# One issue order for the whole kernel, with PSUM banks and elu's buffers named in it, in a fused linear attention and ELU feed-forward kernel

## The chip, the cores and the metric

The kernel runs on one core of one Trainium2 chip. The metric is the device time of one execution in microseconds, taken as the median of several runs. Engines are named as in the profile: PE is TensorE's matmuls, PEld its weight loads, DVE is VectorE, ACT is ScalarE, POOL is GpSimd, SP is SyncE, whose queue issues most DMAs. L704 is line 704 of the kernel before.

## The reference

For four batches of eight heads, 768 steps and a head of 48, a state of 48 x 48 is decayed by row and updated at each step, and read out; the output, as 3072 tokens of 384, goes through a feed-forward layer with ELU. All is float32.

```python
state = alpha[:, :, t, :, None] * state + einsum('bhd,bhe->bhde', k[:, :, t], v[:, :, t])
y[:, :, t] = einsum('bhd,bhde->bhe', q[:, :, t], state)
...
h = x @ w_in                                   # 384 -> 2048
g = where(h > 0, h, exp(minimum(h, 0)) - 1)
out = g @ w_out                                # 2048 -> 384
```

## The kernel before

**Windows.** The attention goes in 24 windows of 128 steps (6 per batch). A window is made by steps with names of their own, called tokens; i is the window. L loads q, k and alpha, LV loads v (both on SP's queue). SC scans alpha into a running product P, LN and EX make its inverse R, KA, KB and KC scale k by it (KC with a Newton step), SQ scales q, PC adds up a check. T (or TP on PE with KN on ACT) transposes k. S multiplies k by q in blocks of 64 steps, MK masks that. U multiplies k by v, UA, UB and UC carry the state (UC's result is the next window's). Y multiplies the state and the masked scores into y; XH rounds y to the upper half in float32r, XL is the rest, and XD moves 32 rows of both by two DMAs into xt, the block's input of the feed-forward.

**Feed-forward.** It goes in 9 blocks of tokens, three of 256 (two windows each) and six of 384 (three windows each), and in 16 parts j of 128 hidden units (8 pairs of parts for the narrow blocks). A(b,j) are the matmuls into a PSUM bank h, nine (or 18) for the three products upper x upper, upper x rest, rest x upper. RA and RB (ACT) make exp(min(h,0)), RC (DVE) the ELU, GH (ACT) its upper half, GL the rest. O(b,j) multiplies both into the two or three output banks, Z copies a bank out on ACT and stores it. A(b,.) needs all of block b's windows, XD too.

**Weights.** F loads a packed weight, DA, KW and DB unpack it, WH and WL split it into upper half and rest. LC, CA and CB load the weights again in small pieces and check them.

**Order.** Each engine and each DMA queue works its instructions in the order in which the tokens are called. That order is a list: START up to block 3, written out (L52), then STEADY (L94), one pattern for a wide block and three windows, which steady() (L830) repeats with shifted numbers. PSUM is eight banks; bank() (L123) takes the bank of the next tile from the string BANKS (L87). The tiles of elu (r, gh, gl) and of the output copy share eleven buffers that the framework hands out (L688, L762). Sets of numbers choose the engine of a step: WLV, KAV, KBV and SQV name the windows or weights whose step runs on VectorE, the others run on GpSimd (L246); inr() (L690) says for which (b,j) RC writes its result to SBUF and GL runs on GpSimd; for the others RC writes over h in PSUM and GL runs on VectorE. At the end a general version stands behind a branch that is not taken; VH gives PE and ACT a hint of where the branch goes (TAIL, L107).

Of the kernel before, what the change touches and what calls it, by code (L numbers as in the profile page):

```python
# [48 lines left out]
START = """  # L52
X.2.0 LA.0 SC.0 LN.0 LB.0 LA.1 SQ.0 EX.0 KA.0 SC.1 KB.0 LB.1 LV.1 LN.1 LV.0 KC.0 TP.0 EX.1 KA.1 KB.1 KC.1 S.0 L.2 SQ.1
KN.0 F.0 U.0 UC.0 PC.0 TP.1 KN.1 SC.2 LN.2 S.1 MK.1 MK.0 U.1 F.2 SQ.2 EX.2 KA.2 UA.0 L.3 UP.1 UC.1 KB.2 PC.1 YL.0 Y3.0
DA.0 X.2.2 Y.0 KC.2 TP.2 LV.2 UA.1 YL.1 F.4 SC.3 S.2 KW.0 DB.0 F.6 XH.0 KN.2 LV.4 Y3.1 U.2 UA.2 Y.1 F.1 LN.3 EX.3 MK.2
YL.2 UB.2 WH.2 WL.2 KA.3 KB.3 XH.1 F.3 Y3.2 F.5 SQ.3 XP.0 XL.0 WH.0 WL.0 XP.1 XL.1 KW.2 KW.1 Y.2 XH.2 DA.2 KC.3 A.0.1
DB.2 WH.4 F.10 WH.6 WL.6 S.3 DA.1 MK.3 TP.3 KN.3 PC.3 A.0.0 LV.3 RA.0.0 U.3 RB.0.0 XP.2 F.8 UC.2 RA.0.1 RB.0.1 UA.3
UB.3 DB.1 L.5 UC.3 DA.4 YL.3 Y3.3 XL.2 A.0.3 WL.4 SC.5 KW.4 WH.1 RC.0.0 Y.3 XH.3 XL.3 A.0.2 L.4 F.7 RC.0.1 A.1.1 WH.3
A.1.0 PC.2 RA.0.3 GH.0.1 WL.3 GH.0.0 SC.4 DA.3 GL.0.0 WL.1 DB.4 KW.3 DB.3 RB.0.3 RA.1.1 RA.0.2 LN.4 RB.0.2 LN.5 RC.0.2
O.0.0 RA.1.0 EX.5 KA.5 RB.1.1 EX.4 RC.1.1 RB.1.0 RC.1.0 F.11 GH.1.1 KA.4 A.1.2 GL.0.1 KB.5 F.12 GH.1.0 A.1.3 GL.1.0  # L60
RA.1.2 RB.1.2 RC.1.2 O.0.1 RC.0.3 WH.8 LC.3 O.1.0 GH.0.2 RA.1.3 WH.5 GH.1.2 GL.0.2 WL.8 GL.1.1 O.1.1 A.0.4 RB.1.3 L.6
RC.1.3 GL.1.2 KC.5 SQ.4 WH.10 TP.5 GH.0.3 GL.0.3 CA.3 GH.1.3 WL.5 O.0.2 RA.0.4 RB.0.4 SQ.5 S.5 CB.3 KB.4 KN.5 KC.4
WH.7 WL.7 F.14 WL.10 F.9 RC.0.4 MK.5 S.4 MK.4 DA.6 KW.6 DA.5 L.8 A.1.5 RA.1.5 RB.1.5 DB.6 O.0.3 PC.5 GH.0.4 RC.1.5
# [989 lines left out]
```

## Time and profile before

| | us |
|---|---|
| median of 3 runs | 468.52 |
| lowest, highest | 467.69, 471.43 |
| the profiled execution: its own time | 470.39 |
| its span, first to last instruction | 468.7 |
| PE busy | 459.6 |
| DVE, ACT, POOL busy | 357.9, 324.5, 163.9 |

The profile is of one execution. A busy PE is not PE at its peak, since matmuls are pipelined; how fast a group of matmuls follows the one ahead is read from the chain that ended last, where a piece runs from the start of its first instruction to the start of the next piece.

### The profile page before, as it was taken

How to read it: one execution, taken by the hardware profiler on the slowest of the kernel's cores; microseconds unless marked ns; L12 is line 12 of the kernel's file. 1: busy time of each engine (PE TensorE's matmuls, PEld its weight loads, DVE VectorE, ACT ScalarE, POOL GpSimd, SP SyncE). 2: the span in 40 equal slices, each digit the busy share in tenths (PEclk: the TensorE clock that was granted, in tenths of full speed). 3: DMA queues.
4: the chain of work that ended last, by engine and by line, in shares of the span. 5: the costliest groups of instructions: out<-in, count | busy, mean ns of one | idle time of the engine just before them, and what ended most of it. 6: DMA issues, size and time to landing. Idle time of an engine off the chain costs nothing.

```text
span 468.7 us, 12508 instructions
## 1 busy us (share of the span) xinstructions
PE 459.6 (98%) x4981; PEld 443.2 (95%) x4982; DVE 357.9 (76%) x780; ACT 324.5 (69%) x736; POOL 163.9 (35%) x145
## 2 busy tenths in 40 slices
...
GB/s 311 395 390 414 111 102 102 229 128 35 163 239 0 66 207 87 143 71 186 113 75 179 77 177 112 161 96 154 90 97 143 40 93 65 52 0 52 2 2 57
DMA packets 22979, 61.10 MB, mean 130 GB/s; under 512 B 2944, under 2 KB 9856, under 8 KB 22912
## 3 DMA queue, kind: packets, MB, share of 16 engines
...
q10 hardware_dynamic: 432, 0.59, 0.3%
...
## 4 chain that ended last, share of the span: by engine, by line
PE 94%; DMA 2%; SPq 1%; DVE 1%; issue 1%; ACT 0%; ACTq 0%
PE o L753 40%; PE h L704 40%; PE y L481 3%; PE q L352 2%; PE y L476 2%; PE q L397 2%; PE wp L152 2%; PE sc L368 1%; DMA vs<-in_vv_dram 1%; PE tp L303 1%; DMA xt<-y 1%; PE y L530 1%; PE yl L476 1%; PE u L415 1%; SPq L578 0%
## 5 line engine op out<-in xcount | busy, mean ns | idle before, releaser
L704 PE MATMUL h<-xt,w 128*128 128x384 f32 (+1 forms) x1296 | 202.6, 310 | 1.0 <-DMA xt<-y 1.0
L704 PEld LDWEIGHTS h<-xt,w 128*128 128x128 f32 x1296 | 191.2, 190 | 2.0 <-PE q L352 1.1
L753 PE MATMUL o<-w,gh 128*128 128x384 f32 x768 | 189.0, 328 | 0.0
L753 PEld LDWEIGHTS o<-w,gh 128*128 128x128 f32 x768 | 133.8, 189 | 0.9
L713 ACT ACTIVATE r<-h 128x384 f32<-128x384 f32 (+1 forms) x120 | 60.9, 514 | 95.8 <-PE h L704 93.4
L753 PE MATMUL o<-w,gl 128*128 128x384 f32 x384 | 125.3, 326 | 0.0
L737 POOL TENSOR_TENSOR gl<-r,gh 128x384 fp32r<-128x384 f32 (+1 forms) x43 | 48.8, 1134 | 169.1 <-ACT gh L730 135.8
L313 DVE STREAM_TRANSPOSE kn<-qka 32x128 f32<-32x128 f32 x256 | 77.3, 302 | 4.0
L753 PEld LDWEIGHTS o<-w,gl 128*128 128x128 f32 x384 | 72.6, 189 | 0.1
L724 DVE SCALAR_TENSOR_TENSOR h<-r,h 128x384 f32<-128x384 f32 (+1 forms) x77 | 42.3, 575 | 34.6 <-ACT r L718 34.2
L718 ACT ACTIVATE r<-r 128x384 f32<-128x384 f32 (+1 forms) x120 | 64.3, 548 | 1.7
L282 POOL TENSOR_TENSOR st<-qka,P 64x512 f32<-64x512 f32 x36 | 44.0, 1221 | 29.6 <-DVE P L230 15.2
L737 DVE TENSOR_TENSOR gl<-h,gh 128x384 fp32r<-128x384 f32 (+1 forms) x77 | 43.1, 574 | 7.6 <-ACT gh L730 6.1
L252 POOL TENSOR_TENSOR qka<-qka,R 128x512 f32<-128x512 f32 x19 | 24.4, 1284 | 58.5 <-ACT R L244 44.3
L730 ACT CAST gh<-h 128x384 fp32r<-128x384 f32 (+1 forms) x77 | 37.0, 495 | 6.7 <-DVE h L724 4.1
L724 DVE SCALAR_TENSOR_TENSOR r<-r,h 128x384 f32<-128x384 f32 (+1 forms) x43 | 25.5, 593 | 20.8 <-ACT r L718 18.2
L380 DVE TENSOR_TENSOR st<-q,mask 64x256 f32<-64x256 f32 x72 | 30.4, 422 | 7.6 <-PE q L397 4.5
L230 DVE TENSOR_TENSOR_SCAN P<-qka,first 128x516 f32<-128x516 f32 x24 | 29.8, 1243 | 1.6 <-DMA qka<-in_qka_dram 0.8
L646 ACT ACTIVATE ck<-ck,lim 128x384 f32<-128x384 int32 x32 | 26.5, 829 | 0.5
L641 ACT ACTIVATE ck<-ck,lim 128x384 int32<-128x384 int8 x32 | 25.7, 804 | 0.0
L730 ACT CAST gh<-r 128x384 fp32r<-128x384 f32 (+1 forms) x43 | 23.3, 544 | 2.7 <-DVE r L724 2.7
L257 POOL TENSOR_TENSOR R<-P,R 128x512 f32<-128x512 f32 x17 | 22.0, 1297 | 1.2
...
## 6 DMA issues: line engine op xcount, KB each, us to landing
...
```

Source lines behind the costliest of these rows:

```text
L230: nc.vector.tensor_tensor_scan(out=P.rearrange("p n w -> p (n w)"), data0=t[:, 2 * NP * W:], data1=first.rearrange("p n w -> p (n w)"), in ...
L282: eng(SQV, i).tensor_tensor(out=st[r, a], in0=d["q"][r], in1=pw(i)[r], op=ALU.mult)
L313: nc.vector.transpose(out=kn[32 * t:32 * t + 32, :, 32 * g:32 * g + 32], in_=d["kt"][32 * g:32 * g + 32, :, 32 * t:32 * t + 32])
L380: nc.vector.tensor_tensor(out=d["st"][r, a, :, c * C:(c + 1) * C], in0=d["s4"][a][o], in1=mask[o].unsqueeze(1).broadcast_to([64, NP, C]), ...
L646: nc.scalar.activation(out=t[:, :, 1].bitcast(F32), in_=t[:, :, 0], func=AF.Square, bias=lim[:, 1:2], accum_out=chk_w[:, f:f + 1])
L704: nc.tensor.matmul(h[:, y, :], lhsT=t[:, wi, ws], rhs=x[:, c, xi].rearrange("p (a x) -> p x a", a=2), start=(y == 0 and k == 0), stop=(k = ...
L713: nc.scalar.activation(out=r, in_=d["h"], func=AF.Relu, scale=-1.0)
L718: nc.scalar.activation(out=d["r"], in_=d["r"], func=AF.Exp, scale=-1.0)
L724: nc.vector.scalar_tensor_tensor(out=d["g"], in0=d["r"], scalar=-1.0, in1=d["h"], op0=ALU.add, op1=ALU.max)
L730: nc.scalar.copy(out=gh, in_=d["g"])
L737: q.tensor_tensor(out=gl, in0=d["g"], in1=d["gh"].bitcast(F32), op=ALU.subtract)
L753: nc.tensor.matmul(o[:, 0:DM], lhsT=gt[:, y, ms], rhs=t[:, wi, f * DM:f * DM + DM].rearrange("p (a x) -> p x a", a=2), start=(u == 0 and y ...
```

## The change

Both lists and steady() go; ORDER is one list of all tokens from the first to the last. BANKS is a new string for it. SLOTS is a new string that names, for each tile of elu and each output copy in the order of their allocation, which of the eleven buffers it takes (ring()). GQ lists the (b,j) whose RC writes to SBUF and whose GL runs on GpSimd, 91 instead of 43. WLV, KAV, KBV and SQV are new. T, MK and Z are called in parts everywhere. At the end Z(8) copies bank 1 first, then comes ACT's hint, then banks 0 and 2; before, the hint came ahead of all three. KW, DA and DB can take half a weight, which ORDER does not use. The matmuls are those of before.

```diff
-WLV, KAV, KBV, SQV = (0, 2, 3, 4, 8, 10, 11, 12), (0, 1, 2, 4, 8), (0, 1, 2, 3, 4, 5, 11), (0, 1, 3)
+WLV, KAV, KBV, SQV = (0, 2, 3, 4, 8, 9, 11, 12, 13),  \
+    (0, 1, 2, 4, 8, 14, 19),  \
+    (0, 1, 2, 11, 15, 17, 19, 22),  \
+    (0, 1, 3, 23)
...
-GQW = (2, 5, 8, 11, 14)
-GQS = ((0, 1), (0, 4), (0, 5), (0, 6), (0, 7), (1, 1), (1, 5), (1, 7), (2, 1), (2, 3), (2, 4), (2, 5), (2, 7))
+GQ = {tuple(map(int, x.split("."))) for x in """
+0.1 0.4 0.5 0.6 0.7 1.1 1.4 1.5 1.7 2.0 2.2 2.3 2.4 2.5 2.6 2.7 3.0 3.1 3.2 3.3 3.4 3.5 3.6 3.7 3.8 3.9 3.10
+3.11 3.13 3.14 3.15 4.0 4.1 4.2 4.3 4.4 4.7 4.8 4.9 4.10 4.11 4.12 4.13 4.14 4.15 5.0 5.1 5.2 5.3 5.4 5.5 5.6
...
+ORDER = """
+LA.0 LB.0 SC.0 SQ.0 LN.0 EX.0 LA.1 SC.1 LB.1 KA.0 LN.1 KB.0 KC.0 EX.1 TP.0 KN.0 PC.0 KA.1 KB.1 S.0 LV.0 L.2 KC.1 PC.1
+SQ.1 U.0 TP.1 KN.1 UC.0 SC.2 SQ.2 LN.2 EX.2 S.1 MK.0 LV.1 U.1 UP.1 MK.1 KA.2 KB.2 KC.2 X.2.2 X.2.0 UA.0 F.2 YL.0 UA.1
...
+RA.3.9 L.12 SC.12 PC.10 RC.3.0 T.11.1 GH.3.0 O.2.5 O.2.6 RB.3.9 LC.4 GL.2.7 T.10.0 A.3.2 LV.10 O.2.7 Z.2.0 RA.3.2
...
+T.18.3 A.5.15 RA.5.15 RB.5.15 RC.5.15 A.5.12 RA.5.12 RB.5.12 O.5.6 RC.5.8 RC.5.9 L.20 GH.5.7 GL.5.7 SQ.19 S.18 GH.5.8
+U.18 Y.17 XH.17 GL.5.8 T.19.1 RC.5.12 GH.5.12 MK.18.1 UA.18 XL.17 O.5.7 LC.18 UB.18 GH.5.11 GL.5.11 A.5.14 GH.5.9
+GL.5.9 A.5.10 LV.19 UC.18 O.5.8 O.5.9 SC.20 T.19.2 SQ.20 CA.18 RB.5.13 CB.18 MK.18.0 U.19 RA.5.10 RB.5.10 RC.5.10
+XD.17 RC.5.13 S.19 UA.19 MK.19.1 GH.5.10 GL.5.10 XD.16 A.6.3 A.6.4 MK.19.0 LN.20 EX.20 KA.20 RA.6.3 KB.20 RA.6.4 A.6.1
...
+MK.23.1 RA.7.1 RB.7.1 Y.21 UA.22 Y.22 XH.22 UB.22 UC.22 XH.21 UA.23 RC.7.1 GH.7.1 Y.23 XL.22 A.7.11 XL.21 XD.21 GL.7.1
...
+GH.8.14 GH.8.12 GL.8.12 GL.8.11 O.8.11 O.8.12 RA.8.15 GL.8.13 RB.8.15 RC.8.15 GH.8.15 GL.8.15 GL.8.14 VH.PE O.8.13
+O.8.15 Z.8.1 VH.Activation Z.8.0 Z.8.2
 """
...
+SLOTS = """
+0123456789a10264587930182a739084526a1456a37290a83758a678a091425a97814629306a5781094350a294619a374053
...
-TAIL = ((("VL",), ("O", NBLK - 1, 8)), (("VH", "PE"), ("O", NBLK - 1, 13)),
-        (("VH", "Activation"), ("Z", NBLK - 1, 0)))
...
+    def ring(dt, name):
+        return gpool.tile([128, 512], dt, name=name, tag=f"g{next(slots)}", bufs=1)
+
     def gtile(b, dt, name):
-        return cut(b, gpool.tile([128, 512], dt, name=name, tag="g", bufs=11))
+        return cut(b, ring(dt, name))
 
     def inr(b, j):
-        return j in GQW if wide(b) else (b, j) in GQS
+        return (b, j) in GQ
...
-            ot = gpool.tile([128, 512], F32, name="ot", tag="g", bufs=11)[:, 0:DM]
+            ot = ring(F32, "ot")[:, 0:DM]
...
-    rest = steady()
-    while rest:
...
+    order = [t.split(".") for t in ORDER.split()]
+    while order:
```

## Rows read from the trace of the kernel before

**Rows 1.** The page's busy times (us, share of the span) and instructions of each engine.

```profile
PE 459.6 (98%) x4981; PEld 443.2 (95%) x4982; DVE 357.9 (76%) x780; ACT 324.5 (69%) x736; POOL 163.9 (35%) x145
```

**Rows 2.** Waits of PE: us in total, times, longest.

```profile
PE h L704 <- DMA xt<-y: 1.0, 1, 1.0
PE sc L368 <- issue: 0.8, 1, 0.8
```

**Rows 3.** The chain that ended last, 200 to 205 us: start, us, what.

```profile
200.08 1.08 PE y L481 x32
201.17 0.50 PE q L397 x32
201.67 0.48 PE q L352 x32
202.15 1.66 PE h L704 x9
203.81 1.46 PE o L753 x9
```

**Rows 4.** The same chain at 174 us: three windows' Y together.

```profile
173.82 2.95 PE y L481 x96
```

**Rows 5.** The same chain at 35 us and from 130 to 135 us.

```profile
35.66 0.35 DVE vs L434
...
130.05 0.59 SPq L219
...
131.39 0.64 SPq L578
...
132.07 3.26 DMA xt<-y
```

**Rows 6.** Y17 and Y20 in the chain, XD's issues on SP, landing of L578.

```profile
290.07 1.08 PE y L481 x32
...
294.80 1.24 SPq L578 DMA_DIRECT2D xt<-y  x2
...
297.03 1.23 SPq L578 DMA_DIRECT2D xt<-y  x2
...
343.77 1.15 PE y L481 x32
...
348.97 1.23 SPq L578 DMA_DIRECT2D xt<-y  x2
...
DMA to landing us min/median/max: 2.1/2.8/4.9
```

**Rows 7.** GL and KB by line (ns min/median/max), and RB on the page.

```profile
L737 DVE TENSOR_TENSOR gl<-h,gh x77: 547/558/749, 46.2 to 458.1; 128x384 fp32r<-128x384 f32 x66, 128x512 fp32r<-128x512 f32 x11
L737 POOL TENSOR_TENSOR gl<-r,gh x43: 1000/1011/2256, 52.2 to 457.3; 128x384 fp32r<-128x384 f32 x30, 128x512 fp32r<-128x512 f32 x13
...
L257 POOL TENSOR_TENSOR R<-P,R x17: 1178/1187/3059, 85.9 to 365.9; 128x512 f32<-128x512 f32 x17
...
L718 ACT ACTIVATE r<-r 128x384 f32<-128x384 f32 (+1 forms) x120 | 64.3, 548 | 1.7
```

**Rows 8.** The end: ACT's last copies and issues, branch and hint, SP's last wait.

```profile
462.91 0.48 ACT L763 COPY ot<-o 128x384 f32<-128x384 f32 x1 [0.50 <-PE o L753]
463.42 0.74 ACTq L766 DMA_DIRECT2D out_dram<-ot  x1
...
464.76 0.34 ACTq L766 DMA_DIRECT2D out_dram<-ot  x1
...
L1047 ACTq BRANCH_PREFETCH_HINT  x1: 50/50/50, 457.2 to 457.2; - x1
...
L869 ACTq COMPARE_BRANCH  x1: 68/68/68, 465.1 to 465.1; - x1
L869 ACTq EVENT_SEMAPHORE  x1: 17/17/17, 467.8 to 467.8; - x1
...
SPq L1047 <- ACTq L869: 0.7, 1, 0.7
```

More of the change, by code (lines that the diff above doesn't have):

```diff
@@ L54 @@
[L54 to L63, printed above, removed]
@@ L333, in KN, with shared @@
         nc.scalar.copy(out=d["kn"], in_=d["tp"].rearrange("p n (a x) -> p n a x", a=2))
-    def shared(i):
+    def shared(i, banks=2):
         d = win[i]
         if i < PAIRS or "q4" not in d:
-            d["q4"] = [bank("q") for _ in range(1 if QU <= i < QS and i % NW == NW - 1 else 2)], set()
+            d["q4"] = [bank("q") for _ in range(banks)], set()
         return d["q4"]
@@ L390, in U4 @@
         d = win[i]
-        q4, begun = shared(i)
+        q4, begun = shared(i, 1 if i < PAIRS and i % NW == NW - 1 else 2)
         d["u"] = [t[:, 0:NP * D].rearrange("p (n e) -> p n e", n=NP) for t in q4]
@@ L600, in F, with words, KW, DA @@
         nc.sync.dma_start(out=to[:, 0:8 * WCH - 3], in_=wgt[f].bitcast(U8)[:, 3:])
[L602 to L609 removed]
+    def words(p, ks):
+        a = slice(ks[0], ks[0] + 1) if ks else slice(0, 2)
+        return raw[p][:, a, :, 0], raw[p][:, a, :, 1], wm[p].bitcast(I32)[:, a]
+    @tok
+    def KW(p, *ks):
+        r = raw[p][:, ks[0]:ks[0] + 1] if ks else raw[p]
+        top = r.rearrange("p a k two -> p (a k two)").bitcast(U8).rearrange("p (x e) -> p x e", e=8)[:, :, 4]
+        nc.scalar.activation(out=r.rearrange("p a k two -> p (a k) two")[:, :, 1], in_=top, func=AF.Copy,
                              scale=1.125, bias=0.5625)
     @tok
[L614 to L615 removed]
+    def DA(p, *ks):
+        if p in wm:
+            pass
+        elif p % 3 == 0 or p == NJ - 1:
             wm[p] = work.tile([128, 2, WCH], F32, name="wm", tag="wm", bufs=1)
@@ L809, in VH @@
                                      engines=[getattr(mybir.EngineType, e) for e in engines])
-    start = [t.split(".") for t in START.split()]
-    with tc.manual_schedule():
-        for name, *at in start:
-            TOK[name](*map(int, at))
-    rest = steady()
-    while rest:
-        at = [x[0] == "VH" for x in rest].index(True) if any(x[0] == "VH" for x in rest) else len(rest)
+    order = [t.split(".") for t in ORDER.split()]
+    while order:
+        cut_at = next((k for k, x in enumerate(order) if x[0] == "VH"), len(order))
```

178 lines of the change are left out of this document (96 added, 82 removed), and 2 rows, old and new, of the table GQ.

## The prediction

> **What bounds the kernel now.** I read the busy times first, then the waits of TensorE (PE), then the chain that ended last, then the ends of the span. The busy line says PE is busy 459.6 of 468.7 us [rows 1], so whatever ends anywhere must show as an idle PE or as PE work that takes longer than it must. Once PE has begun, its waits are few: 1.0 us before a matmul of A that waited for a transfer into xt, 0.8 us of "issue" inside S [rows 2]; and 3.9 us lie behind the last output's issue at 464.76 [rows 8]. The rest of what can be won is in the chain: a group of nine A matmuls or nine O matmuls takes 1.46 us when its neighbours are A or O too, but 1.66 us when it is the first behind a visit to the attention's small matmuls [rows 3]. So a visit costs 0.20 us more than its own pieces, and the pieces depend on the neighbours: 32 Y matmuls alone take 1.08 us [rows 3], 96 in one go 2.95 us [rows 4], so each further Y beside a Y costs (2.95 - 1.08) / 2 = 0.935. VectorE, ScalarE and GpSimd (POOL) have slack in the mean (76%, 69%, 35% of the span [rows 1]).
>
> **What the change does, part by part.** The matmuls are the same in number, shape and kind (the tokens of PE in both orders are the same set; VP and the warm-up X included), so PE's own floor does not move. Five things can move the end.
>
> 1. Fewer visits. From the first A on, the order of before leaves A/O 33 times for something else, the new one 27 times (counted in the two orders). Priced from rows: a visit of S, U and Y is 1.08 + 0.50 + 0.48 + 0.20 = 2.26 us [rows 3], one of S and U 0.98 + 0.20 = 1.18, of Y alone 1.08 + 0.20 = 1.28, of three Y 2.95 + 0.20 = 3.15 [rows 4]. At the end of the attention, (Y21 U22 S22), (S23 U23 Y22), (Y23) cost 2.26 + 2.26 + 1.28 = 5.80 and become (U22 S22 S23 U23), (Y21 Y22 Y23), 1.18 + 0.98 + 3.15 = 5.31: 0.49 less. Y15 and Y18 go from beside S/U (2.26 - 1.18 = 1.08) to beside another Y (0.935): 0.145 each, 0.29. (Y7 Y8), 1.28 + 0.935 = 2.21, joins Y6 and costs 1.87: 0.34 less. S3 with TP3 goes ahead of the first A: one refill, 0.20. TP4, TP6 and TP9 go beside S, Y and Y: about 0.1 in all. Sum 1.4 us. Bounds: 1.1 (the first three alone) and 2.4 (six visits at 0.40, the refill and as much again for entering).
>
> 2. The wait at block 3. XD(8), two transfers into xt, is issued at 131.39 and 132.07, behind the two transfers of LV(10) (0.59 us each), and the last lands 3.26 us later; A(3,0) waits for it [rows 2, 5]. Before, Y8 and A(3,0) have O, O, TP, A, U, S between them; in the new order TP9, A, O, O, U, S, O, A, A stand between Y8 and A(3,1), and LV(10) is behind XD(8). That is three more groups of 1.95 to 2.0 us of PE work: the wait of 1.0 us goes, and what is late next is 5 us away. Minus 1.0, bounds 0 and minus 1.0.
>
> 3. The same wait elsewhere. In the wide part before, Y stands early, and nothing waits. In the new order A(6,3) follows Y17 after five groups and U19, S19: 5 x 1.46 + 0.20 + 0.98 = 8.5 us; A(7,2) follows Y20 after five groups: 7.5 us. What the path needs can be read from before. Y17 ended at 291.15; XD(17)'s pair was issued from 294.80 to 296.04, XD(15)'s from 297.03 to 298.26; Y20 ended at 344.92 and XD(20)'s pair was issued from 348.97 to 350.20; a transfer lands 2.1 us to 4.9 us (median 2.8) after its issue [rows 6]. Taking the median from the second issue (half a pair, 0.6 us, before the pair's end), the own transfer is there 291.15 -> 298.2, 7.1 us after Y17, and 344.92 -> 352.4, 7.5 us after Y20; the pair behind it 2.2 us later, 9.3. In the new order XD(16) stands behind XD(17), so A(6,3) needs up to 9.3 and has 8.5: a wait up to 0.8; with a slower issue 1.6. A(7,2) needs 7.5 and has 7.5: 0 to 0.6. I take 0.9 for both. Lower bound 0 (the vector work between Y and XD may be earlier in the new order), upper 2.2, or 6.4 if both land at the 4.9 of the longest row.
>
> 4. Elementwise steps. The set GQ names 91 (b,j) for GL on POOL, where before 43 ran there; 57 are new, 9 go back. On POOL a GL takes 1.01 us (median; 2.26 at worst), on VectorE 0.56 [rows 7]. POOL gains 48 x 1.01, about 50 us, on its 163.9, VectorE loses 48 x 0.56 = 27 us of its 357.9 [rows 1, 7]; KA, KB, SQ and WL, moved by the window, change each engine by under 8 us. Against PE this costs nothing while O has time: counted in the order at 1.46 us for a wide group [rows 3], the shortest path from A to its O leaves 4.3 us of PE work (O(3,7), O(8,4)), before 5.85, and the median grows from 15.8 to 19.4 us. RA, RB, RC and GH at RB's 0.55 each [rows 7], a GL of 1.0 and the hand-overs, estimated at 0.3 in all, need about 3.5 us, so the cover is 0.8 us, and a GL of 2.26 would open a wait of 0.5 there. I take 0. With RC written to SBUF the PSUM bank of h is free one or two steps earlier: no wait of PE for a bank is seen before, so 0 too. Where POOL takes longer is seen in its KB: 1.19 median, 3.06 once [rows 7]. The Trainium skill ("SBUF — State Buffer", "Who interferes with whom") states that a VectorE instruction with two SBUF inputs and a GpSimd instruction that reads SBUF exclude each other for the whole instruction; the two maxima agree with it, and by it twice as many GLs on POOL would meet such a block about twice as often.
>
> 5. The ends. At the start X.2.0 is moved from before TP0 to behind UP1: the two warm-up matmuls cost the same there, 0. At the end ScalarE copies o[1] first, then the hint, then o[0] and o[2]. Before, the copy of o[1] began at 462.91, its DMA issue took 0.74 us, the last copy had to wait for that, and the last issue began at 464.76 [rows 8]. Now o[1]'s copy begins at the same time, and two more copies (0.48 each) and two issues (0.34 to 0.74 each) stand between it and the last issue: that is at 465.15 to 465.5, 0.4 to 0.75 later. Against it stands the hint: ScalarE's hint came at 457.2, its branch at 465.1, and the first instruction behind it at 467.8, and the queue that ends the program waited 0.7 us for that one [rows 8], so the hint of before brought nothing. If the later one works, that 0.7 goes and the end is 0.3 earlier; if not, 0.4 to 0.75 later. I take plus 0.1. The Trainium skill ("Runtime: NRT & Kernel Launch", "Instruction fetch mechanics") says that a taken branch to a target outside the two pages held waits for a fetch; the 2.7 us agree, and by that rule a hint nearer to its branch has the better chance.
>
> The 0.84 us of "issue" in S [rows 2] I leave as it is (bounds: gone, or doubled since S3 now comes sooner behind Y2). Load order: the weights' and windows' transfers change places within a few of each other while the queue is full; PE waited for none of them before, and I count 0.
>
> Sum: -1.4 - 1.0 + 0.9 + 0 + 0.1 = -1.4 us. The profiled execution has a span of 468.7 and its own time was 470.4, against a median of 468.5 (467.7 to 471.4) over three runs; the difference is taken from the median: 467.1.
>
> **The rivals.** *All waits gone.* Six visits at 0.40, the 1.0, the 0.84 and a short wait of 0.35 on VectorE at 35.7 [rows 5] gone, no new wait, the end 0.3 earlier: -2.4 - 1.0 - 0.84 - 0.35 - 0.3 = -4.9, 463.6. For it: the lead from A to O grows in the median (part 4). Against: an order that packs closer trades them, as at A(6,3). *One for one.* What goes at A(3,0) and the visits comes back at A(6,3), A(7,2) and at Y23, which stands right behind its state update: 468.5. *Late transfers.* Part 3 at its upper bound with long landings: -1.4 + 1.3 to -1.4 + 5.5, 468.4 to 472.6. *POOL becomes the supplier that PE waits for (slower).* In the new order 30 O whose GL runs on POOL stand right behind that GL, before 11. POOL works in order; a GL that waits for its GH holds the KA, KB and SQ of the next window behind it, and the next GL too. If at a third of the 30 places O waits the 0.45 that POOL is longer, and at three the 1.25 of a blocked one, that is 4.5 + 3.8 = 8.3 us: 475.4. It decides from the point where POOL is no longer idle before its GLs. Against it: before, POOL waited for GH before most of them, its load goes only from 35% to about 45%, and none of the 11 made PE wait.
>
> **How the numbers follow.** Chances: forecast 0.36 (its own range 465.3 to 468.6), one for one 0.20, late transfers 0.14, all waits gone 0.17, POOL 0.13. Predicted is 467.1. For 8 in 10 the range reaches from 463.6 to 471.8; outside are the half of the first rival that does still better, 0.08, and nearly all of POOL's, 0.12. A change of about 1%, 4.7 us, is what these runs can tell from none: under 463.8 is faster, over 473.2 slower. Only "all waits gone" reaches the first, 0.17; POOL the second, 0.13; the rest 0.70.
>
> **What would show it.** PE busy within 2 us of 459.6 and 27 visits; no wait before A(3,1) (part 2); a wait for a transfer into xt before A(6,3) or A(7,2) of 0 to 1.6 us (part 3); POOL's busy time about 210 us, VectorE's about 335, no PE wait on gl (part 4); the gap behind ScalarE's branch under 1 us or still 2.6 (part 5). It is wrong if PE shows more than 4 us of new waits, above all on gl from POOL, or if the visits cost as much as before.

## The result, and the profile after

The changed kernel is slower: median 474.71 us (473.46 to 475.37, 4 runs) against 468.42 (467.69 to 471.43, 4 runs) for the kernel before, a ratio of 1.0119, 95% interval 1.0096 to 1.0142. That is 6.3 us more, 7.6 above the 467.1 predicted and outside the range. A ratio is not the quotient of the two medians beside it, and differs from that by up to 0.2%.

The page of after, busy times and instructions of each engine, answers [rows 1]:

```profile
PE 458.7 (97%) x4981; PEld 442.1 (93%) x4982; DVE 350.3 (74%) x738; ACT 327.9 (69%) x736; POOL 208.0 (44%) x187
```

PE and POOL (208 for 210 predicted) are as forecast, DVE gave up only 8 us of the 23 expected. The span is 473.6 us for 468.7 while PE is busy 0.9 us less, so the loss lies in waits. Those of PE after, of 0.5 us or more, answering [rows 2] (engine and line that waited, what it waited for: us in total, times, longest):

```profile
PE wp L205 <- DVE first L199: 2.1, 1, 2.1
PE tp L356 <- issue: 1.4, 1, 1.4
PE o L813 <- POOL gl L797: 1.3, 2, 0.7
PE sc L421 <- issue: 1.3, 1, 1.3
PE y L529 <- issue: 1.2, 1, 1.2
PE tp L356 <- PE h L764: 0.8, 1, 0.8
PE sc L421 <- DVE gl L797: 0.8, 1, 0.8
```

The first stands in both kernels. Not one of the others is a wait the prediction priced, and the two of before are gone. To know which belong to the kernel and which to one execution, both kernels were profiled again.

> The kernel before, unchanged, for a second profile: its first profile was of an execution of 470.4, while its runs lie at 468.6. Theory: the 1.8 us lie in the first 20 us, where the first loads land (the kernel that begins with the same 214 tokens reached the same work there 1.0 us earlier), and from there on both profiles agree within 0.3 us. Rival: the 1.8 us are spread over the whole span.

> The changed kernel, unchanged, on the same chip and in the same rounds as the experiments: 474.7 as before, ratio 1.012 to 1.014; a second profile shows the same waits (1.4 before TP.0, 1.2 in Y.1, 1.3 in S.3, 0.8 before TP.5, 0.8 before S.5, 0.8 and 0.9 at 333 and 435 us), each within 0.3 us.

Before: 468.69 (468.07 to 469.36), profiled span 466.9. After: 473.95 (473.62 to 475.04), span 471.9, ratio 1.0129 [1.0114, 1.0145] to before's runs beside it (median 468.33). The only wait of PE in the second profile of before, then those of 0.5 us or more in that of after (the wait of 2.1 again, and these):

```profile
PE wp L152 <- DVE first L146: 2.1, 1, 2.1
```

```profile
PE sc L421 <- issue: 1.5, 1, 1.5
PE o L813 <- POOL gl L797: 1.3, 2, 0.7
PE y L529 <- issue: 1.2, 1, 1.2
PE sc L421 <- DVE gl L797: 0.8, 1, 0.8
PE tp L356 <- PE h L764: 0.8, 1, 0.8
```

The two waits of [rows 2] that the prediction worked with did not come back, so they belonged to that one execution; the waits of after come back, except for TP0's 1.4.

Where the time goes is seen by setting executions side by side at equal work: the columns of PE's matmuls added up at 2.4 GHz (439 us in all) serve as a clock, and the lag of an execution is its time at a given sum less that of the second profile of before at the same sum. Worked out from the matmul records, us:

```
work of PE, us       10     20     30     60    110    160    300    330    390    440
before, 1st       -0.14  -0.18   0.69   0.78   0.75   1.75   1.76   1.79   1.78   1.57
after, 1st         0.86   3.80   2.86   4.97   5.34   5.25   4.83   5.97   5.32   6.07
after, 2nd        -1.36   1.90   0.96   2.98   3.35   3.26   2.92   3.95   3.30   4.26
e3 buffers         0.18   3.17   2.23   4.25   4.63   4.53   4.47   4.59   3.94   3.94
e4 start           -1.22   0.32   0.03   0.78   1.84   1.75   1.91   2.95   2.30   3.26
e8 O(0,2)          0.87   3.81   2.87   3.04   4.90   4.81   4.69   5.83   5.18   5.93
e12 LV4           -0.33   2.04   2.33   4.37   4.73   4.75   4.47   5.61   4.95   5.71
e14 seam          -0.85  -0.73  -1.01  -1.05  -1.08   1.33   0.96   1.18   0.53   0.31
e16 seam          -0.71  -0.18  -0.47  -0.43   1.03   2.87   7.64   7.76   7.11   7.11
```

A column's own value depends on chance at the start (the first column scatters by 2 us within one order); the steps along a row depend on it much less. From 10 to 60 us of work after loses 4.3 (2nd) or 4.1 (1st), and five other profiles with its start, but for one step or one engine set (e1, e3, e6, e9, e11), lose 4.0 to 4.1; with before's start five profiles lie between a gain of 0.2 and a loss of 0.9, and a sixth loses 2.0 (e4, below). Further on, from 60 to 160 after loses about 0.3, from 160 to 300 it gains 0.3 to 0.4, from 300 to 330 it loses 1.0 to 1.1, to 390 it gains 0.65, to 440 it loses 0.8 to 1.0. From the start of the last matmul to the end of the span it is 5.7 us against 4.95 in the second profiles, 0.7 more (5.6 against 5.1 in the first, 0.4).

### The profile page after: what moved, and what is told of

The parts are those of the page before. It is cut to its first block, busy times and chain, and to the rows that moved or that the text cites. A ratio compares the mean times of both kernels' runs of the same rounds, so it can differ in the third digit from the quotient of the medians.

```text
span 473.6 us, 12516 instructions
## 1 busy us (share of the span) xinstructions
PE 458.7 (97%) x4981; PEld 442.1 (93%) x4982; DVE 350.3 (74%) x738; ACT 327.9 (69%) x736; POOL 208.0 (44%) x187
## 4 chain that ended last, share of the span: by engine, by line
PE 94%; issue 1%; POOL 1%; DMA 1%; DVE 1%; ACT 0%; ACTq 0%; POOLq 0%; SPq 0%
PE h L764 39%; PE o L813 39%; PE y L534 4%; PE q L450 2%; PE y L529 2%; PE q L405 2%; PE wp L205 2%; PE sc L421 1%; PE tp L356 1%; DMA qka<-in_qka_dram 1%; PE y L583 1%; POOL gl L797 1%; PE u L468 1%; POOL st L335 1%; PE yl L529 0%
## 5 line engine op out<-in xcount | busy, mean ns | idle before, releaser
L797 POOL TENSOR_TENSOR gl<-r,gh 128x384 fp32r<-128x384 f32 (+1 forms) x91 | 98.8, 1090 | 176.5 <-ACT gh L790 126.8
L784 DVE SCALAR_TENSOR_TENSOR r<-r,h 128x384 f32<-128x384 f32 (+1 forms) x91 | 51.0, 575 | 38.7 <-ACT r L778 29.8
L790 ACT CAST gh<-r 128x384 fp32r<-128x384 f32 (+1 forms) x91 | 46.8, 528 | 17.0 <-DVE r L784 12.8
L335 POOL TENSOR_TENSOR st<-qka,P 64x512 f32<-64x512 f32 x34 | 42.9, 1261 | 4.6 <-DVE P L283 2.5
L283 DVE TENSOR_TENSOR_SCAN P<-qka,first 128x516 f32<-128x516 f32 x24 | 32.3, 1345 | 3.5 <-DMA qka<-in_qka_dram 3.0
L784 DVE SCALAR_TENSOR_TENSOR h<-r,h 128x384 f32<-128x384 f32 (+1 forms) x29 | 17.1, 597 | 21.6 <-ACT r L778 21.3
L292 ACT ACTIVATE R<-P 128x512 f32<-128x512 f32 x24 | 15.1, 631 | 18.3 <-DVE P L283 18.3
L315 DVE SCALAR_TENSOR_TENSOR qka<-R,qka 128x512 f32<-128x512 f32 x24 | 23.1, 961 | 4.2 <-POOL R L310 3.7
L797 DVE TENSOR_TENSOR gl<-h,gh 128x384 fp32r<-128x384 f32 (+1 forms) x29 | 17.0, 590 | 11.9 <-ACT gh L790 6.1
## 6 DMA issues: line engine op xcount, KB each, us to landing
vs<-in_vv_dram SPq DMA_DIRECT2D x6, 384.0 KB, 11.5
```

What stands on the lines that cost most here:

```text
L283: nc.vector.tensor_tensor_scan(out=P.rearrange("p n w -> p (n w)"), data0=t[:, 2 * NP * W:], data1=first.rearrange("p n w -> p (n w)"), in ...
L335: eng(SQV, i).tensor_tensor(out=st[r, a], in0=d["q"][r], in1=pw(i)[r], op=ALU.mult)
L784: nc.vector.scalar_tensor_tensor(out=d["g"], in0=d["r"], scalar=-1.0, in1=d["h"], op0=ALU.add, op1=ALU.max)
L790: nc.scalar.copy(out=gh, in_=d["g"])
L797: q.tensor_tensor(out=gl, in0=d["g"], in1=d["gh"].bitcast(F32), op=ALU.subtract)
```

## The experiments

Each edit is of the changed kernel's ORDER unless it says otherwise; "..." is what stands between. Before was run again beside each; its medians there are 468.1 to 468.8.

**Which part holds the loss.** The first 214 tokens of before (to about 66 us), then the changed order:

```diff
-LA.0 LB.0 SC.0 SQ.0 LN.0 EX.0 LA.1 SC.1 ...
+X.2.0 LA.0 SC.0 LN.0 LB.0 LA.1 ...
```

> The first 214 tokens of the order of before (up to RA(0,4), about 66 us), their PSUM banks and engines with them, then the rest of the changed kernel's order with its banks and buffers. Theory 'start': the changed kernel is 4.2 us behind at the same work at 70 us, and all of it goes: 470.5, which leaves the end (0.4 us), the waits at 333 and 435 us (1.7) and the shorter visits (about minus 1.5). Rival 'POOL' (the GL moved to GpSimd cost all along the kernel): 1 to 2 us less at most, 473. Rival 'one for one' (the rest of the order only works behind its own start, and VectorE is behind at 70 us here too): 474.7.

472.07 (471.46 to 472.72), ratio 1.0076 [1.0063, 1.0089]: 1.9 to 2.6 us back. Its lag moves from -1.22 at 10 us to 0.78 at 60, a loss of 2.0 in place of 4.3; what it has left at the start is one wait of 1.3 in Y1, which is 0 to 0.3 in the other five profiles with before's start (before twice, e13, e14, e16). By the medians a third to two fifths of the loss is won back; by the lags of those five the start of after costs more, 3.2 to 4.5.

**What PE waits for in the first 30 us.** Before's SC(1) stood behind KA(0); the changed kernel has it earlier:

```diff
-EX.0 LA.1 SC.1 LB.1 KA.0
+EX.0 LA.1 LB.1 KA.0 SC.1
```

> The changed kernel with one token moved: SC.1, the scan of window 1, stands behind KA.0 on VectorE again, as in the kernel before. In the changed kernel the scan waited until 7.8 us for its load and held KA.0, KB.0 and KC.0 behind it, and the first transposes TP.0 waited 1.4 us for KC.0. Theory 'start' (most of the loss lies in the first 70 us, each wait by itself): TP.0 starts 1.2 us earlier and the kernel takes 1.2 us less, 473.5. Rival 'given back' (a later stage, the supply of TensorE's instructions at 25 and 31 us or VectorE at 60 us, sets the time at 70 us anyway): TP.0 is earlier by as much, but at 70 us 0 to 0.4 us of it is left, 474.3 to 474.7.

473.77 (472.05 to 474.81), 1.0115 [1.0098, 1.0133]: nothing. The second profile of after, without this edit, has the same lag as this one, within 0.03, from 20 to 60 us of work. The 1.4 us before TP0 were chance: in the other profiles that wait lies anywhere from 0 to 2.2.

The two waits by "issue" wait for no semaphore. PE in the second profile of after (start, us, engine, line, operation, tiles, count, idle time before):

```profile
22.06 0.84 PE L529 MATMUL y<-st,vs 48*48 48x64 f32 x23
24.06 0.93 PE L529 MATMUL y<-st,vs 64*48 64x64 f32 x25 [1.16 <-issue]
...
28.10 0.90 PE L421 MATMUL sc<-st,qka 48*64 48x64 f32 x24
30.52 0.45 PE L421 MATMUL sc<-st,qka 48*64 48x64 f32 x8 [1.52 <-issue]
```

They break Y1 and S3 in the middle, near PE's 704th and 960th instruction (256 apart; a few records are missing, so the count is near). The page lists a DMA queue q8 of kind "instruction": 41 transfers, 0.67 MB, 16 KB each. That they carry PE's program is read from their number (41 x 256 = 10496; 10090 instructions of PE are on record) and from the two places. The table sets the landing of two of them, by the DMA records, beside the time at which PE was 256 instructions ahead of the break. That a transfer falls due there is an assumption, taken from the spacing (us):

```
                          2nd transfer                    3rd transfer
                  PE at 448  landed  stall in Y1   PE at 704  landed  stall in S3
before, 1st         19.48     21.74     0            23.67     29.95     0.84
before, 2nd         19.88     22.37     0            24.08     29.30     0
e4 before's start   18.67     23.06     1.3          22.87     29.37     0
after, 2nd          18.21     22.71     1.2          22.68     29.14     1.5
e5 LV4 behind F3    18.57     22.92     0.9          23.05     30.77     3.2
e12 LV4 behind Y0   18.96     20.57     0            23.44     26.41     0
```

Where PE stalls, it goes on 1.2 to 1.5 us after the transfer's landing (24.06 after 22.71, 30.52 after 29.14). In the first profile of before the same thing happened in S3: it landed at 29.95 and PE went on at 31.36. That was the 0.8 of "issue" in [rows 2]. The theory from this: the instruction transfer stands in the DMA engines behind weights, and the new load order has the engines full when it is asked for. In S3 something else comes in: the third transfer took 5.2 to 6.3 us in before too (6.5 in after), but there A(0,1) stood ahead of S3, and PE had 6.6 us from 704 to the break; in after it had 6.1, and of those 1.2 are the stall in Y1. The rival: a fixed cost of the step in the code, whatever the loads. Three places for LV(4), which waits on SP for its buffer and holds the weights behind it, tell them apart:

```diff
-L.4 LC.3 LV.4
+LV.2 F.6 LV.4
```

> The changed kernel with one token moved: LV.4, the load of v of window 4, stands behind F.6 and ahead of F.4 on SyncE's queue. It must wait for a buffer until about 20 us, and so the weight loads F.4, F.3, F.1 are issued some 5 us later, as in the kernel before. Theory 'supply' (the 1.2 us without a releaser in Y.1 at 24.8 us are TensorE's own instructions, which arrive late because weight loads fill the transfer engines): that gap falls below 0.3 us, 1.2 us less, 473.5. Rival 'place' (the gap belongs to the place in the program and not to the loads): it stays at 1.2, 474.7. Rival 'weights late' (the loads delayed make DA, DB, WH of block 0 late): the gap goes, but A(0,.) waits as long, 474.7 or more.

In this one LV(4) overwrites window 0's values while Y0 still reads them; the instructions and their shapes stay. Times fell in two groups, 473.0 to 474.0 and 477.5 to 481.5; median 474.02, 1.0104 [1.0089, 1.0119]. The profile is of the second group and shows something else. By stretch: its length, the busy time of PE, weight load, DVE, ACT, POOL, then the granted clock, DMA share and GB/s:

```profile
8.00:10.00 2.00, 1.11 (x6) 0.29 (x3) 1.97 (x3) 0.76 (x2) 0.00 (x0) 1.00 1.02 414
10.00:12.00 2.00, 0.69 (x6) 0.55 (x8) 1.93 (x4) 0.62 (x3) 0.00 (x0) 0.98 1.02 419
12.00:14.00 2.00, 2.00 (x36) 1.88 (x38) 1.83 (x3) 1.89 (x5) 0.00 (x0) 0.50 1.01 424
```

PE idled for much of four us (2.2 in one piece before TP0, which stands ahead of the edit), and then ran at 0.50, the 1.2 GHz level, until 24 us. It does not answer the question, since PE comes to Y1 at another pace.

> The changed kernel with one token moved: LV.4, the load of v of window 4, stands behind F.3 on SyncE's queue, ahead of F.1, F.10 and F.8. It waits there for Y.0, until about 24 us, so at 20 to 24 us the transfer engines have less queued than in the changed kernel. Theory 'supply': TensorE's instructions, asked for at 20.2 us, arrive 2 to 3 us later and not 4.6, and the gap of 1.2 us in Y.1 goes; that in S.3 goes or stays, since the loads held back are then queued: 0.5 to 1.5 us less, 473.2 to 474.2. Rival 'place': the gap in Y.1 stays at 1.2; 474.7. Rival 'weights late': block 0's weights come late and A(0,.) or A(1,.) waits for them by as much as 3 us: 475 to 477.

474.70 (473.87 to 476.99), 1.0132 [1.0116, 1.0147], not told from after by its median. In its profile, of the slowest execution, S3 stalls for 3.2 where the third transfer took 7.7 us from due to landing. The rival has no reason for 3.2.

> The changed kernel with LV.4 right behind Y.0, so that SyncE's queue holds F.4 and all later loads back until Y.0 is done at about 22 us; at 18 to 22 us the transfer engines run dry, as in the kernel before, whose LV.4 holds them back until 20 us. Theory 'supply': TensorE's next instructions, asked for at 18 to 20 us, land 2 to 2.5 us later as in the kernel before (2.3 and 2.5) and not 4.5, and the gap of 1.2 us in Y.1 goes. What that brings in all is open: later loads come 4 to 6 us later, and A(0,.) or A(1,.) may wait for weights: 473 to 476. Rival 'place': the gap in Y.1 stays at 1.2 with an empty queue.

473.73 (472.27 to 474.99), 1.0097 [1.008, 1.0114]. The mechanism is shown: both stalls are gone, and e4 above has before's order and the stall in Y1, with a transfer that took 4.4 us. The same columns as above, the second profile of after, then this kernel:

```profile
18.00:20.00 2.00, 2.00 (x44) 1.76 (x41) 1.96 (x4) 2.00 (x4) 0.00 (x0) 1.00 1.02 421
20.00:22.00 2.00, 2.00 (x82) 2.00 (x79) 1.87 (x3) 1.97 (x7) 0.61 (x1) 1.00 1.04 420
```

```profile
18.00:20.00 2.00, 2.00 (x53) 1.76 (x49) 1.97 (x4) 1.77 (x3) 0.00 (x0) 1.00 0.49 199
20.00:22.00 2.00, 2.00 (x72) 2.00 (x75) 2.00 (x2) 1.97 (x6) 0.00 (x0) 1.00 0.00 0
```

With the engines empty the transfer landed 1.6 us after it fell due, with them full 4.5. But the gain was taken back at once, by XL(0), the rest of y for xt, which ACT has not written when A(0,1) comes (10 to 60 us of work lose 4.7):

```profile
PE h L762 <- ACT xt L620: 1.6, 1, 1.6
```

XL(0) ahead of XL(1) and KW(2) as well:

```diff
-F.3 TP.3 XL.0 WL.2
+F.4 XP.1 XL.0 XL.1 ... F.3 TP.3 WL.2
```

> e12 with one token moved: XL.0, which makes the second half of block 0's input on ScalarE, stands ahead of XL.1, before KW.2 (1.8 us) and XH.2. In e12 neither Y.1 nor S.3 had a gap, and A(0,1) waited 1.85 us for XL.0. Theory 'ScalarE's order': the wait goes, and at 35 us the kernel is at +0.5 us against the second profile of before and not at +2.3; the time is 1.8 us less than e12's, 472.0. Rival 'pace' (ScalarE and VectorE are full from 20 to 70 us and set the time at 70 us whatever is moved): a wait before U.3, A(1,.) or TP.5 grows by as much: 473.7.

474.45 (472.19 to 475.95), 1.0128 [1.0106, 1.015]. That wait is gone too, and then U3 waits for v, whose load SP now issues later:

```profile
PE q L448 <- DMA vs<-in_vv_dram: 2.1, 1, 2.1
```

In this profile TP5 and S5 (below) do not wait either, and 10 to 60 us of work lose 1.5 in place of 4.3. But the profiled execution, 472.19, is the fastest of four, and the other three (474.3 to 476.0) do not share its gain: an inconclusive run on the size, clear on what comes next. The other way round, S3 behind the first A, where the third transfer has landed (three banks renamed as well):

```diff
-KB.3 KC.3 S.3 F.3 TP.3 XL.0 WL.2 DA.2 KN.3 DB.2 A.0.1
+KB.3 KC.3 F.3 XL.0 WL.2 DA.2 DB.2 A.0.1 S.3 TP.3 KN.3
```

> The changed kernel with S.3, TP.3 and KN.3 behind A(0,1) again, as in the kernel before (three tokens moved, nothing else). Theory 'supply': TensorE runs through 256 small instructions in 4.7 us there, and the next part of its program, asked for at 22.7 us, lands at 29.1 us behind queued weight loads; A(0,1) puts 2.0 us of large matmuls in between, and in the kernel before, where it does, the second profile shows no gap. The gap of 1.3 to 1.7 us in S.3 goes, and the one in Y.1 (1.2) stays: 1.3 to 1.5 us less, 472.6. Rival 'weights late': A(0,1) then waits for its weight (WL.2) and nothing is gained, 474.0. Rival 'given back' (VectorE sets the time at 62 us, TP.5 and S.5 wait for it): the gap goes and the waits before TP.5 and S.5 grow by as much, 474.0.

475.17 (472.58 to 476.09), 1.0131 [1.011, 1.0152]: no gain. The stall in S3 is gone, and in its place A waits 0.8 for ACT's xt and U3 0.7 for KN(3).

**The banks at 62 to 66 us.** In the second profile of after TP5 and S5 wait for DVE: by BANKS they take the banks of h(1,2) and h(1,3), which GL(1,2) and GL(1,3) read last. For TP5 the profile names PE's own h, which ended at 61.73; the GL ended at 62.40. L315 is KC, L732 WL, L332 SQ:

```profile
60.08 1.72 DVE L315 SCALAR_TENSOR_TENSOR qka<-R,qka 128x512 f32<-128x512 f32 x1
61.21 1.63 POOL L332 TENSOR_TENSOR st<-qka,P 128x512 f32<-128x512 f32 x1
61.72 0.68 DVE L797 TENSOR_TENSOR gl<-h,gh 128x512 fp32r<-128x512 f32 x1
...
62.50 0.63 PE L356 MATMUL tp<-ident,qka 128*128 128x128 f32 x4 [0.76 <-PE h L764]
62.80 1.82 POOL L732 TENSOR_TENSOR w<-spare,w 128x768 fp32r<-128x768 f32 x1
62.92 2.25 DVE L315 SCALAR_TENSOR_TENSOR qka<-R,qka 128x512 f32<-128x512 f32 x1
...
65.92 0.29 PE L421 MATMUL sc<-st,qka 48*64 48x64 f32 x3 [0.83 <-DVE gl L797]
```

More work of other kinds ahead of them:

```diff
-GH.1.3 WL.5 TP.5 ... RC.1.5 WH.12 O.0.2
+GH.1.3 WL.5 O.0.2 TP.5 ... RC.1.5 WH.12
```

> The changed kernel with O(0,2) moved ahead of TP.5 (it stood 15 us later). Theory 'bank': TP.5 and S.5 wait 0.8 us each since their PSUM banks are those of h(1,2) and h(1,3), which VectorE's GL frees late; 2.0 us of other work in between, whose gh and gl are ready at 60 us, cover both: 1.6 us less, 472.4. Rival 'VectorE sets the pace' (VectorE is busy without a pause from 50 to 70 us): the waits move to MK.5, KN.5 or the next O, and at 75 us nothing is gained: 474.0.

473.63 (472.51 to 475.43), 1.0103 [1.0089, 1.0117]. Both waits are gone, 10 to 60 us of work lose 2.2 in place of 4.3; then A waits 1.2 for DVE's state update, and from 60 to 110 it loses 1.9 in place of 0.4. By the lag from 10 to 110 us 0.4 to 0.7 stays, and the medians do not tell that from nothing.

Was it POOL that held DVE back? KB(3), KB(4), KB(5) on DVE again:

```diff
-KBV: 0 1 2 11 15 17 19 22
+KBV: 0 1 2 3 4 5 11 15 17 19 22
```

> The changed kernel with KB of windows 3, 4 and 5 on VectorE again, as before (one set changed, nothing else). In the changed kernel VectorE's KA.4, KC.5 and KC.4 at 57 to 67 us took 1.7, 1.7 and 2.3 us, where in the kernel before KC of windows 5 and 4 took 1.1 and 0.7; while they ran GpSimd worked on KB, SQ and WL. Theory 'exclusion' (GpSimd's KB keep VectorE out): these three fall below 1.2 us, VectorE is earlier at GL(1,2) and GL(1,3), and TensorE's waits before TP.5 and S.5 fall from 1.6 us together to under 0.6: 1 us less, 473. Rival 'load' (VectorE has too much to do from 50 to 70 us whoever does KB): it gets 0.7 us per KB later, and the waits grow: 474.5 to 475.5.

474.12 (473.92 to 475.83), 1.0125 [1.0106, 1.0144]: TP5's wait falls to 0.4, S5's rises to 1.3. POOL's KB is not the cause. That POOL plays no part is not shown: beside POOL's SQ and WL the two KCs ahead of these GLs took 1.72 and 2.25 us, in e11 still 1.71 and 2.25, where the second profile of before has 1.14 and about 0.7. No run takes SQ and WL off POOL there. Over the whole kernel 13 of the 48 KC and SC are more than 0.15 us over their medians in the second profile of after (1.0 to 2.25 us, where the medians are 0.69 and 1.23), 6 in that of before, and POOL was working beside every one of them. With the 57 GLs back on VectorE (e6, next) there are 7.

**Is POOL the supplier that PE waits for?** The 57 GLs back on VectorE, with RC still to SBUF and the order kept:

```diff
-        q = nc.gpsimd if inr(b, j) else nc.vector
+        q = nc.gpsimd if inr(b, j) and was(b, j) else nc.vector
```

> The changed kernel with GL of the 57 (b,j) that the change moved to GpSimd on VectorE again (RC still writes to SBUF, the order and all buffers stay): VectorE gets 57 x 0.56 = 32 us more, GpSimd 57 x 1.09 = 62 us less. Theory 'start and buffers': only TensorE's waits on a GL from GpSimd change, 0.3 us at 201 us gone and those at 333 and 435 us shorter by the 0.45 that VectorE is quicker: 0.5 to 1.2 us less, 473.5 to 474.2. Rival 'POOL' (GpSimd as supplier costs all along, or slows VectorE by excluding it from SBUF): 2 us less or more, under 472.7. Rival 'VectorE full': VectorE, which is 95% busy or more from 50 to 90 us, gets later there: 475.5 or more.

516.61 (513.47 to 519.89), 1.1038 [1.0999, 1.1077]: 42 us slower than after. Where PE waits most:

```profile
PE o L817 <- DVE gl L801: 22.6, 12, 4.3
```

So this order needs these GLs on POOL. Apart from the two waits of the next part, the price of POOL to PE at its GLs is small: once, in O at 200 us, PE pauses 0.27, where SQ's two instructions (L335) stand ahead of a GL. The chain that ended last, second profile of after:

```profile
196.54 1.19 POOL st L335
...
197.79 1.20 POOL st L335
...
199.05 1.02 POOL gl L797
...
200.11 4.33 PE o L813 x25
```

**The buffers of elu.** PE's 1.3 on gl are O(6,1) and O(8,1). After, first profile; in the brackets how long POOL sat idle before the GL, and whom it waited for:

```profile
332.88 2.08 POOL L797 TENSOR_TENSOR gl<-r,gh 128x384 fp32r<-128x384 f32 x2 [2.30 <-PE o L813]
...
333.94 0.43 PE L813 MATMUL o<-w,gl 128*128 128x384 f32 x1 [0.65 <-POOL gl L797]
...
434.86 1.00 POOL L797 TENSOR_TENSOR gl<-r,gh 128x384 fp32r<-128x384 f32 x1 [13.14 <-PE o L813]
...
435.92 0.43 PE L813 MATMUL o<-w,gl 128*128 128x384 f32 x1 [0.70 <-POOL gl L797]
```

POOL was idle for 2.3 and for 13.1 us, and what released it is an O. SLOTS gives GL(6,1) the buffer of gh(6,0) and GL(8,1) that of gh(8,0), which O(6,0) and O(8,0) just ahead were still reading. Their own GHs were done at 316.9 and 432.9. The edit swaps two GLs, puts one RA behind, and names the buffers anew:

```diff
-A.6.5 RA.6.5 GL.6.7 ... UC.20 O.6.0 GL.6.1
+A.6.5 RA.6.5 GL.6.1 ... UC.20 O.6.0 GL.6.7
...
-RC.8.11 A.8.5 RA.8.5 ... GH.8.1 GL.8.1
+RC.8.11 A.8.5 ... GH.8.1 GL.8.1 RA.8.5
```

> The changed kernel with its order and buffer names changed at two places: GL(6,1) and GL(6,7) change places, and RA(8,5) stands behind GL(8,1), so that GL(6,1) and GL(8,1) take a buffer that has long been free and not the one that O(6,0) or O(8,0) just ahead of them still reads. Theory 'buffers' (TensorE's waits of 0.81 and 0.87 us at 333 and 435 us come from eleven buffers that are all taken): both waits go, 1.7 us less, 473.0. Rival 'POOL' (GpSimd is late since it has twice as many GL): both waits stay, or appear at the next GL, 474.7.

472.30 (471.03 to 473.29), 1.0075 [1.0062, 1.0088]: 1.7 to 2.4 us less than after's two medians, 1.9 by the lag (300 to 330: 0.12 for 1.03; 390 to 440: 0 for 0.96). Neither wait is left on its page. Of the mended waits of PE it is the only one whose whole gain stayed.

**The end, and Y6 earlier.** Before's end (hint, then banks 0, 1, 2), and ZV(6), Y(6) ahead of U(8), in which PE waits 0.5 in two pieces (two banks renamed for it):

```diff
-U.8 LN.9 ... ZV.6 ... Y.6
+ZV.6 Y.6 U.8 LN.9 ...
...
-O.8.13 O.8.15 Z.8.1 VH.Activation Z.8.0
+O.8.13 O.8.15 VH.Activation Z.8.0 Z.8.1
```

> The changed kernel with two edits far apart, each read by its place. First, the end of before: ACT's hint ahead of Z(8), which copies the banks in the order 0, 1, 2. From the last matmul to the end of the span it is 4.95 us in the kernel before and 5.68 in the changed one; theory: 0.5 to 0.7 us less, and the hint costs nothing at either place; rival: the 0.7 us are chance, and it stays within 0.2. Second, Y.6 ahead of U.8: U.8 waits 0.8 us for a bank that MK.8 frees late, since a scan on VectorE took 2.2 us instead of 1.2; theory: the wait goes, 0.8 us less; rival: Y.6 or Y.7 then waits instead. Together 472.5 to 473.5.

475.77 (473.92 to 476.21), 1.0140 [1.0122, 1.0158]. The end is 0.8 shorter (4.83 us behind the last matmul for 5.6 to 5.7). Y6 was a miss: the lag grows by 3.2 from 100 to 110 us, where after's grows by 0.9; TP9 now waits 1.6 and Y 0.8 for st.

> The changed kernel with S.3 behind A(0,1), O(0,2) ahead of TP.5, Y.6 ahead of U.8, the two buffer edits of e3 and the end of before. If the losses are separate waits, each with its own place, they add up: 1.4 + 1.6 + 0.8 + 1.7 + 0.6 = 6.1 us less than 474.0, 467.9, as fast as the kernel before or 0.5 us faster. Rival 'one for one' (what is gained early is given back at a later wait): half of it or less, 471.

e3, e7, e8 and e9 in one: 475.02 (474.81 to 475.34), 1.0139 [1.0125, 1.0154]. Not all of the four had won something: e7 had not, and e9's Y6 lost 2.3, which comes back here (3.2 from 100 to 110 us of work). The buffers' gain stays (from 160 to 440 us of work it gains 0.9, where after loses 1.0). What e8 won early is given back to the next supplier that is late (A waits 1.3 for DVE's state and 0.8 for ACT's xt, U3 0.7 for ACT's kn, Y 0.8 for DVE's st).

**Before's start with the changed rest.** The first 466 tokens of before (to about 135 us), then the changed order with e3's edits and before's end:

> The first 466 tokens of the order of before (to A(3,0), about 135 us) with their engines, then the changed kernel's order with its banks and buffers, the two buffer edits of e3 and the end of before. Theory 'places' (the changed kernel loses in its first 130 us, by full buffers at two places and at its end, and its wide part is shorter by what its fewer visits save): level with the second profile of before at 130 us, 0.4 us ahead of it at the last matmul, the same from there: 468.0, as fast as the kernel before or a little faster. Rival 'engine sets' (twice as many GL on GpSimd cost TensorE all along the wide part): 469.5 or more.

474.59 (474.31 to 475.58), 1.0133 [1.0116, 1.015]. The seam itself spoils it: the changed order has RC(2,6) late, and A(2,7) waits for its bank. Timeline, then stretches as above (granted clock the third figure from the end):

```profile
141.38 7.56 PE L759 MATMUL h<-xt,w 128*128 128x256 f32 x36 [4.28 <-DVE r L779]
```

```profile
138.00:141.00 3.00, 0.00 (x0) 0.00 (x0) 2.86 (x7) 1.98 (x6) 2.15 (x2) 0.76 0.57 182
141.00:145.00 4.00, 3.62 (x17) 3.65 (x18) 1.35 (x5) 0.00 (x0) 1.74 (x2) 0.50 0.40 163
```

```diff
-MK.9 A.3.0 ... T.11.3 RC.2.6 T.11.0 A.2.7
+RC.2.6 MK.9 A.3.0 ... T.11.3 T.11.0 A.2.7
```

> e13 with one token moved: RC(2,6) ahead of MK.9 on VectorE, where the order of before has it ahead of the scan SC.10. In e13 the seam between the two orders had put it behind the scan and KB, KC and T of window 11, A(2,7) waited 4.45 us for its bank, and TensorE's clock fell for a stretch behind that. Apart from it e13 was 0.7 us ahead of the kernel before at 126 us and gained 1.0 us more from 134 us to the end. Theory 'places': both gains show now, 467.4, 1 us faster than the kernel before. Rival: A(2,7) or A(3,1) still waits 1 us or more at the seam: 468.5.

469.28 (468.28 to 471.1, 12 runs), 1.0017 [1.0003, 1.0031]: as fast as before within 1%, in fact 0.5 (medians) to 0.8 us (ratio) behind. By its lag the seam costs 2.4 (110 to 160), and from 160 to 440 us this kernel gains 1.0 on before (e13 1.1; before's first profile gains 0.2 on its second). So the changed wide part is the better one by 0.8 to 1.1 us in these profiles, once its buffers are right. To get at that gain, the seam at another place (416 tokens, 118 us), and the weights' checks LC, CA, CB of the two orders moved to where both agree:

> The order of before for its first 416 tokens (up to A(2,3), about 118 us), then the changed order with the two buffer edits of e3 and the end of before; the checks LC, CA.5 and CB.5 moved behind CB.15, CA.0 and CB.0 behind O.2.1. Theory (the start of before is worth its 2.7 us, the wide part from 160 us on with its buffers mended is about 1 us shorter than before's, and only the seam of e13 and e14 cost): 467.5, about 1 us faster than before. Rival (any seam between the two orders costs 1 us or more, since what the one has done ahead is not what the other takes for done): 468.5 to 469.5, no change from before.

476.04 (475.18 to 476.74), 1.0173 [1.0158, 1.0188]. The seam cost 3.3 (60 to 160 us) here, and one of the moved checks 4.8 more: ACT, which makes gh, sat behind a transfer for it.

```profile
273.71 0.63 ACT L693 ACTIVATE ck<-ck,lim 128x384 int32<-128x384 int8 x1 [3.19 <-DMA ck<-in_wgt_dram]
...
275.55 0.59 PE L808 MATMUL o<-w,gh 128*128 128x384 f32 x2 [2.64 <-ACT gh L785]
```

```profile
276.00:278.00 2.00, 1.52 (x5) 1.37 (x5) 0.76 (x2) 1.94 (x7) 1.71 (x2) 0.56 0.88 293
```

From 300 to 440 us it gains 0.5 on before, e14 0.65. No kernel here beats before; whether a join without a seam would keep that gain stays open.

## Why the prediction was wrong, point by point

**Visits (part 1): right.** The second profiles show 33 and 27 visits, as counted. From 160 to 440 us of work the visits, with the first two matmuls behind each, take 0.58 us more than their columns at 2.4 GHz in before, and 0.68 less in after: 1.26 saved. The pauses of PE at the two buffers are 0.81 and 0.87, the one behind SQ is 0.27, and the matmul behind each of the three comes 0.11 late as well: -1.26 + 1.95 + 0.32 = +1.0, and the lag from 160 to 440 us grows by 1.00. Of the forecast -1.4 most was there, in that part, and it was covered.

**The wait at block 3 (part 2): failed, -1.0 that could not be won.** A(3,1) does not wait, as said, but neither does A(3,0) in before's second profile. [rows 2] came from an execution 1.9 us above the median, and its two waits, 1.0 and 0.84, make up those 1.9. The sum took off the 1.0, and applied it to the median, from which these waits are already gone: the 1.0 was counted twice.

**Late transfers (part 3): failed in size, +0.9 that did not come.** A(6,3) came 8.4 us after Y17 (8.5 forecast), and the path was shorter. Second profile of after; Y17 ended at 295.87:

```profile
297.61 2.60 SPq L631 DMA_DIRECT2D xt<-y  x4
...
304.29 0.92 PE L764 MATMUL h<-xt,w 128*128 128x384 f32 x4
```

XD is issued 1.7 us after Y17, in [rows 6] it was 3.7. In before DVE had MK, KC and a GL ahead of XL(17), which began at 293.97, 1.6 us after XH(17) was done; in after it began right behind XH(17), at 296.79. So the 3.7 held other work of before's order, and the estimate carried it over as if it were the steps' own time. The lower bound, 0, had named this case.

**Elementwise steps (part 4): the GL itself nearly right (0.3 for 0), the buffers left out (+1.7), the banks wrong (+1.6).** "No wait of PE for a bank is seen before, so 0 too" fell at TP5 and S5, 0.8 each. Buffers of elu had no term at all, though SLOTS was named in the diff: which buffer a GL takes decides whose O it waits for, in a queue that is in order. Over the whole kernel POOL's GLs wait for an O 14 times:

```profile
L797 POOL TENSOR_TENSOR gl<-r,gh x91: 993/1009/1816, 45.8 to 462.2; 128x384 fp32r<-128x384 f32 x75, 128x512 fp32r<-128x512 f32 x16
...
  PE o L813: 40.8, 14
```

In before it was 4 times, 11.5 us in all. VectorE lost the 27 us of GL as forecast. By the durations of the single instructions, second profiles, 5.6 came back in KC and SC, the same 48, lengthened beside POOL (6 of them in before, 13 in after), and some 8 in KA, WL, SQ, DA and DB, in part because there are more of them. The prediction's "about twice as often" came out, and its cost fell on DVE.

**The ends (part 5): +0.1 was +0.4 to +0.7, the upper bound.** Second profile of after, the first of ACT's last copies, the last issue, ACT's hint and branch, and SP's last wait:

```profile
465.60 0.48 ACT L823 COPY ot<-o 128x384 f32<-128x384 f32 x1 [4.48 <-PE o L813]
...
468.03 0.34 ACTq L826 DMA_DIRECT2D out_dram<-ot  x1
```

```profile
L1069 ACTq BRANCH_PREFETCH_HINT  x1: 50/50/50, 466.5 to 466.5; - x1
...
L891 ACTq COMPARE_BRANCH  x1: 68/68/68, 468.4 to 468.4; - x1
L891 ACTq EVENT_SEMAPHORE  x1: 17/17/17, 471.0 to 471.0; - x1
...
SPq L1069 <- ACTq L891: 0.7, 1, 0.7
```

The first instruction behind the branch comes 2.6 us later, as before (463.4 to 466.0 there; 2.7 in [rows 8]), and SP waits 0.7 as in [rows 8]. The hint 1.9 us ahead of the branch won nothing; the copies behind it were left.

**Issue in S, and the load order: failed, and the largest.** "PE waited for none of them before, and I count 0." This is the step that failed: the load order, put at nothing, cost 2.7 us. PE waited for no weight; but the loads share the engines with PE's instructions, and S3's 0.84, left "as it is", was that wait. Its upper bound, doubled, would have covered S3's 1.5; Y1's 1.2 had no term. With TP5 and S5 (1.6, the banks put at nothing in part 4) the stalls add up to 4.3 us, what the order loses from 10 to 60 us of work (0.6 more is lost by 20 and 0.9 won back by 30, where other matmuls stand). Mending one wait at a time moved it to another place (e7, e8, e12); in e15's one profile more stayed. Why is argued only: ACT and DVE have little to spare there. The first 70 us of the second profile of after, columns as above:

```profile
0.00:70.00 70.00, 63.48 (x905) 55.74 (x906) 62.06 (x76) 53.66 (x100) 27.13 (x28) 1.00 0.79 289
```

DVE is busy 62 of 70 us there: the mean slack of [rows 1] is not that stretch's slack. But it is 61.9 in the second profile of before as well, where PE waits for nothing behind its first matmul: a full DVE alone does not make the waits.

**The rivals.** POOL's 475.4 was near the time, but not by its mechanism: PE waits 1.3 us on gl where it said 8.3, and that through two named buffers. With the 57 GLs back on VectorE the kernel takes 516.6. The "late transfer" that came was PE's own program, which no rival named. In sum, from 10 us of work to the end, second profiles: +4.3 (start), +0.4 (60 to 110, U8), -0.1 (to 160), +1.0 (wide: visits, buffers, POOL), +0.7 (end) = 6.3, as the first pair of medians differ; the second profile of after was 1.4 ahead at 10 us, by chance (the profiles with its start lie from 1.4 ahead to 0.9 behind there), so that its span is only 5.0 longer.
